# A fused attention and routed expert kernel on one core: k and v of the attention stage loaded as two partition halves, kv products over 128 rows, x written behind all loads

## The chip, the cores and the metric

The kernel runs on one core of one Trainium2 chip. The metric is device time in microseconds (us) of one execution; lower is better. The matmul engine is called PE, VectorE DVE, ScalarE ACT, GpSimd POOL and the queue that issues most DMAs SP.

## The reference

```python
# q, k, v: (8 batches, 8 heads, 576 rows, 64), float32
kv  = einsum('bhsd,bhse->bhde', k, v)          # one 64x64 matrix per batch and head
out = einsum('bhsd,bhde->bhse', q, kv)
rms = sqrt(mean(out * out, axis=-1) + 1e-06)
x   = (out / rms * g_norm) as rows of (4608, 512)      # a row per batch and place, heads side by side
logits = x @ w_gate                            # 8 experts
# greedy, largest logit first: each token goes to one expert, each expert takes 576 tokens
out[mask_e] = relu(x[mask_e] @ w1[e]) @ w2[e]
```

## The kernel before

The program has two stages with a search between them. The attention stage computes x and the logits, the search finds the first expert's threshold, and the expert stage runs two matmul layers for each of the eight experts. The change touches the attention stage alone (lines 69 to 565).

**Loads.** For each batch b and each half h of the heads, `load` (L82) brings k, v and q as one DMA of 576 KB each, so there are 48 loads. A tile holds 128 partitions: two heads of 64 partitions, nine rows of 64 values in each partition (2304 contiguous bytes). k and v of a head thus lie in 64 partitions, and a product over a head's 576 rows is nine matmuls of 64 rows. All loads go through SP; `paced` (L74) makes each wait until the third DMA before it has landed. Every tile has two buffers, so batch b+2 is asked for when batch b has been used (`again`, L398). The first twelve loads come in the order k v q k v q, twice.

**Per batch.** `prepare(b)` (L367) is a generator that is advanced between the output tiles of the batch before. It sums k^T v in `sum_kv` (L391, matmuls L395), copies the odd half out (L415), adds it to the even half (L417), copies kv into both partition halves of `kvx` on POOL (L423), transposes kv (L431, copy L433), multiplies it with the gate's weights (L442, eight matmuls of 64 weight columns, so that an output tile's logits come out of the same matmul as the tile), and turns q with PE transposes (`turn_q`, L376, matmuls L380, copies L384 and L386).

**Output tiles.** `tiles` (L453) makes four tiles of 128 rows for an even batch and five for an odd one, the fifth from two batches. For each, `one` (L464) runs eight matmuls (L479; sixteen for the fifth), ACT squares (L485) and copies (L486), DVE sums (L490). Then `scale` (L492) and `logits` (L500) finish the batch; POOL scales x (L511), for the last five tiles ACT does so at the stage's end in eight pieces per tile (L516).

**Writes.** x goes back to memory through the same SP queue and the same pacing (L520). Writes are held in a list, and a batch's end issues those that are over eight (L557); the rest stands at the end of the stage.

**Order.** The order of instructions on PE, DVE, ACT and SP is the order in which the code calls them. Small DVE jobs for the search ("chores") are placed between tiles (L545, L555). `ones` (L356) are matmuls of a 128x512 bf16 block whose result is not used; they stand at the stage's start (18), before each batch's kv (2), before the first tile (1) and before the fourth (2).

Of the kernel before, what the change touches and what calls it, by code (L numbers as in the profile page):

```python
# [7 lines left out]
FT = mybir.dt.float32  # L8
# [3 lines left out]
AL = mybir.AluOpType  # L12
# [3 lines left out]
P = 128  # L16
# [10 lines left out]
def kernel(  # L27
# [41 lines left out]

    loaded = {}  # L70
    AHEAD = 3
    issued = []

    def paced(dma):  # L74

        if len(issued) >= AHEAD:
            tc.add_manual_dep(dma.ins, issued[-AHEAD].name,
                              mybir.DependencyInfo(mybir.DependencyClass.Sync, mybir.DependencyReason.DATA),
                              reason="paced loads")
        issued.append(dma.ins)  # L80

    def load(name, b, h):  # L82

        loaded[name, b, h] = att.tile([P, NP // 2, R, D], FT, name=f"{name}_sb", tag=name + str(h), bufs=2)
        rs = slice(h * NP // 2, (h + 1) * NP // 2)
        src = {"k": k, "v": v, "q": q}[name]
        paced(nc.sync.dma_start(
            loaded[name, b, h].rearrange("p r j d -> p r (j d)"),
            src[b].rearrange("h s d -> (h s) d").rearrange("(r p j) d -> p r (j d)", r=NP, j=R)[:, rs]))

    for b in range(2):
        for h in range(2):
            for name in "kvq":
                load(name, b, h)

    ones_b = asg.tile([P, P], BF, name="ones_b")
    nc.vector.memset(ones_b, 1.0)
# [269 lines left out]
    def prepare(b):  # L367

        k_sb, v_sb, q_sb = ([loaded.pop((name, b, h)) for h in range(2)] for name in "kvq")
        q_sb = [x.rearrange("p r j d -> p (r j d)") for x in q_sb]  # L370
        NT = NP * R // 2
        qt = att.tile([P, 2, NT, HP], FT, name="qt", tag="qt", bufs=3)
        turned_q[b] = qt

        def turn_q(n):
            m = min(4, NT - 4 * n)  # L376
            t_ps = psa.tile([P, 4, P], FT, name="qt_ps", tag="tr", bufs=2)
            for x in range(m):
                h, at = divmod(4 * n + x, NT // 2)
                nc.tensor.transpose(t_ps[:, x, :], q_sb[h][:, at * P:(at + 1) * P], ident)  # L380

            to, got = qt[:, :, 4 * n:4 * n + m], t_ps[:, 0:m].rearrange("p x (l c) -> p l x c", l=2)
            if n in (1, 2):
                nc.vector.tensor_copy(to, got)  # L384
            else:
                nc.scalar.copy(to, got)  # L386


        kv_ps = psa.tile([P, 2, 512], FT, name="kv_ps", tag="kv")

        def sum_kv(r):  # L391
            for j in range(R):
                for l in range(2):
                    ls, cs = slice(l * D, (l + 1) * D), slice(j % 2 * D, (j % 2 + 1) * D)
                    nc.tensor.matmul(kv_ps[cs, l, r * D:(r + 1) * D], lhsT=k_sb[r // 2][ls, r % 2, j, :], rhs=v_sb[r // 2][ls, r % 2, j, :],  # L395
                                     start=(j < 2), stop=(j >= R - 2))

        def again(names, h):  # L398
            if b + 2 < B:
                for name in names:  # L400
                    load(name, b + 2, h)

        if b > 0:
            ones(2, kv_ps[:, 0, :])
        for r in range(2):
            sum_kv(r)
            if r:
                again("kv", 0)
            turn_q(r)
            yield  # L410
        sum_kv(2)
        sum_kv(3)
        again("kv", 1)
        odd = att.tile([D, 2, NP * D], FT, name="odd", tag="odd")
        nc.scalar.copy(odd, kv_ps[D:P, :, 0:NP * D])  # L415
        kv = att.tile([D, NP, 2, D], FT, name="kv", tag="kv")
        nc.vector.tensor_tensor(kv.rearrange("p r l d -> p l r d"),  # L417
                                kv_ps[0:D, :, 0:NP * D].rearrange("p l (r d) -> p l r d", d=D),
                                odd.rearrange("p l (r d) -> p l r d", d=D), op=AL.add)

        kvx = att.tile([P, H, W], FT, name="kvx", tag="kvx", bufs=3)
# [5 lines left out]
        turn_q(2)  # L427
        again("q", 0)
# [3 lines left out]
        kvt = att.tile([P, NP, D], FT, name="kvt", tag="kvt")  # L432
        nc.scalar.copy(kvt, t_ps)  # L433
        yield
        turn_q(3)
        if b == 0:
            nc.vector.tensor_scalar(gw.rearrange("p r l e -> p (r l e)"), in0=gw.rearrange("p r l e -> p (r l e)"),
                                    scalar1=g_col, scalar2=None, op0=AL.mult)
        w_ps = psa.tile([P, NP, 2 * E], FT, name="w_ps", tag="tr", bufs=2)
        for r in range(NP):  # L440
            for n in range(2):
                nc.tensor.matmul(w_ps[n * D:(n + 1) * D, r], lhsT=kvt[:, r, :],  # L442
                                 rhs=gw[:, r].rearrange("p l e -> p (l e)"), start=True, stop=True)
        nc.vector.tensor_copy(kvx[:, :, D:W], w_ps.rearrange("p r (l e) -> p (r l) e", l=2))
        kv_of[b] = kvx
        turn_q(4)
        again("q", 1)

    LAG = 4
    writes, late = [], []  # L450
    last_own = GC - (R + 1) // 2

    def tiles(c0, rows):  # L453


        T = len(rows)
        o_sb = att.tile([P, T, H, W], FT, name="o_sb", tag="o_sb", bufs=2)
        xo = att.tile([P, T, H, D], FT, name="xo", tag="xo", bufs=LAG + 1)
# [5 lines left out]
        def one(t, copies, fill):  # L464

            o_ps = psa.tile([P, 2, 512], FT, name="o_ps", tag="o", bufs=2)
            ones(fill, o_ps[:, 0, :])
            for r2 in range(NP // 2):
                for l in range(2):
                    for rp in range(2):  # L470
                        r = 2 * r2 + rp
                        at = [slice(h * HP, (h + 1) * HP) for h in range(2)]
                        halves = rows[t]
                        parts = [(slice(0, P), halves[0], 2)] if halves[0][0] == halves[1][0] else [
                            (at[n], half, 1) for n, half in enumerate(halves)]
                        for rows_at, (bn, j), m in parts:
                            block = R * r + j
                            ks = slice(block % 2 * D, (block % 2 + 1) * D)
                            nc.tensor.matmul(  # L479
                                o_ps[rows_at, rp, (2 * r2 + l) * W:(2 * r2 + l + 1) * W],  # L480
                                lhsT=turned_q[bn][ks, l, block // 2:block // 2 + m].rearrange("p x c -> p (x c)"),
                                rhs=kv_of[bn][ks, 2 * r + l], start=True, stop=True)
# [4 lines left out]
            if own or t != T - 2:  # L487
# [41 lines left out]
    with tc.manual_schedule(engines={PE, DVE, ACTE, SPE}):  # L529
# [3 lines left out]
        for b in range(B):  # L533
# [715 lines left out]
```

## Time and profile before

| | |
|---|---|
| median of 3 runs | 661.99 us (658.17 to 667.01) |
| the profiled execution | 660.36 us |
| its span on the core | 658.6 us |
| attention stage, start to its last output matmuls | about 0 to 123 us |
| search, first product with L646 to the expert's weights (L828) | 127.9 to 151.0 us |
| PE busy over the span | 605.8 us (92%) |
| k, v, q loads | 48 of 576 KB, median 5.8 to 6.1 us from issue to landing |
| writes of x | 16 of 512 KB and 4 of 256 KB, 4.4 and 4.0 us |

The time outside the span is 660.36 - 658.6 = 1.8 us. The stretches of ten microseconds show how the engines share the attention stage: the columns are PE, PE's weight loads, DVE, ACT and POOL busy, with counts, then the granted clock, the DMA engines' busy share and the rate.

```profile
50.00:60.00 10.00, 9.37 (x203) 7.53 (x199) 5.02 (x10) 5.80 (x12) 5.07 (x6) 1.00 0.91 294
100.00:110.00 10.00, 8.60 (x210) 7.04 (x208) 8.03 (x14) 5.46 (x11) 6.58 (x7) 1.00 0.96 362
110.00:120.00 10.00, 6.52 (x89) 5.15 (x89) 8.22 (x17) 4.48 (x11) 4.25 (x4) 0.93 0.90 336
120.00:130.00 10.00, 2.69 (x69) 2.32 (x69) 7.37 (x29) 7.90 (x29) 0.00 (x0) 0.50 0.12 49
```

PE and the DMA engines are both nearly full until 110 us. From 120 us on both are nearly idle, and the granted clock is half.

### The profile page before, as it was taken

The page shows a single profiled execution, that of the slowest core. Times are in us where ns is not written, and L with a number is a line of the kernel's source. Part 1 is how long each engine was busy: PE and PEld are TensorE (multiplying, and loading weights), DVE is VectorE, ACT ScalarE, POOL GpSimd, SP SyncE. Part 2 cuts the span into 40 slices and gives each one's busy share as a digit, 9 for nine tenths or more (in the row PEclk, how much of TensorE's full clock was granted, in tenths as well). Part 3 has the DMA queues.
Part 4 walks back from the last instruction along what each step waited for, and adds up shares of the span by engine and source line. Part 5 has one row for each costly group of instructions (what it writes and reads, how often), then busy time and mean ns, then how long its engine had stood idle before and what let it go on. Part 6 is the DMA issues. An engine that isn't in the chain of part 4 may idle for free.

```text
span 658.6 us, 12759 instructions
## 1 busy us (share of the span) xinstructions
PE 605.8 (92%) x4932; PEld 464.6 (71%) x4932; DVE 387.8 (59%) x1249; ACT 194.5 (30%) x395; POOL 389.3 (59%) x405
## 2 busy tenths in 40 slices
PE   7989998335899999999999999999999999999994
PEld 4767777232678677867786786778678867877873
DVE  4466667778678588668757956976671053123201
ACT  1555665611131223123212222231223123222300
POOL 1035434104585487749846974887388669848822
PEclk9999999657999999999999999999999999999998
DMA  8999989416306402710442072109103620721001
GB/s 270 310 315 295 292 291 340 154 50 199 128 0 204 164 33 71 257 41 33 158 171 73 1 262 99 41 0 323 46 32 100 229 72 1 279 84 37 0 9 64
DMA packets 49852, 91.02 MB, mean 138 GB/s; under 512 B 3712, under 2 KB 20096, under 8 KB 49792
## 3 DMA queue, kind: packets, MB, share of 16 engines
q1 hardware_dynamic: 43200, 71.31, 31.6%
q0 software_dynamic: 5888, 18.88, 8.3%
q8 instruction: 39, 0.64, 0.4%
q14 instruction: 21, 0.17, 0.1%
q10 hardware_dynamic: 704, 0.02, 0.1%
HBM read 71.32 MB, written 18.87 MB: 137 GB/s over the span
## 4 chain that ended last, share of the span: by engine, by line
PE 77%; DVE 9%; DMA 5%; issue 4%; ACT 3%; POOL 1%; POOLq 0%; SPq 0%; DVEq 0%; ACTq 0%
PE x_ps L1065 13%; PE x_ps L1025 11%; PE z_ps L1065 9%; PE y_ps L1065 9%; PE z_ps L1025 7%; PE y_ps L1025 7%; PE o_ps L479 4%; PE y_ps L1127 4%; PE kv_ps L395 3%; PE t_ps L969 3%; PE qt_ps L380 2%; DMA v_sb<-in_v_dram 2%; DMA q_sb<-in_q_dram 2%; PE given_ps L651 1%; PE given_ps L646 1%
## 5 line engine op out<-in xcount | busy, mean ns | idle before, releaser
L1070 ACT COPY h<-x_ps 128x288 f32<-128x288 f32 x93 | 37.2, 400 | 166.5 <-PE x_ps L1065 153.7
L1065 PE MATMUL x_ps<-xs,sw 128*128 128x288 f32 x248 | 71.3, 409 | 0.0
L875 POOL DMA_INDIRECT xg<-x_dram,ids x40 | 38.1, 952 | 51.8 <-DMA w_sb<-in_moe_w_dram 37.7
L992 POOL DMA_INDIRECT out_dram<-y_sb,outs x32 | 31.5, 983 | 55.8 <-DVE y_sb L1163 41.1
L1025 PE MATMUL x_ps<-tw,sh 128*128 128x256 f32 x256 | 61.6, 384 | 0.0
L972 ACT ACTIVATE xt<-t_ps,g_col 128x512 f32<-128x512 f32 (+1 forms) x40 | 25.7, 645 | 110.9 <-PE t_ps L969 110.9
L1065 PEld LDWEIGHTS x_ps<-xs,sw 128*128 128x128 f32 x248 | 46.2, 190 | 14.3 <-issue 1.7
L955 POOL TENSOR_TENSOR sw<-w_sb 128x256 f32<-128x256 f32 x64 | 46.8, 731 | 12.3 <-PE z_ps L1065 9.6
L1017 POOL TENSOR_TENSOR sh<-hid 128x512 f32<-128x512 f32 x32 | 40.7, 1272 | 19.9 <-ACT hid L1040 19.9
L1025 PEld LDWEIGHTS x_ps<-tw,sh 128*128 128x128 f32 x256 | 46.9, 190 | 7.1 <-issue 0.8
L1040 ACT ACTIVATE hid<-hid 128x576 f32<-128x576 f32 x64 | 43.8, 686 | 22.9 <-DVE hid L1079 13.1
L511 POOL TENSOR_TENSOR xo<-o_sb,inv 128x512 f32<-128x512 f32 x31 | 32.9, 1090 | 29.7 <-DVE inv L498 16.6
L1103 POOL TENSOR_TENSOR tw<-w_sb 128x512 f32<-128x512 f32 x32 | 40.1, 1276 | 5.0 <-DMA w_sb<-in_moe_w_dram 5.0
L479 PEld LDWEIGHTS o_ps<-kvx,qt 64*128 64x128 f32 (+1 forms) x640 | 33.7, 181 | 12.0 <-issue 7.1
L479 PE MATMUL o_ps<-kvx,qt 64*128 64x72 f32 (+1 forms) x640 | 38.9, 274 | 3.4 <-ACT o_sb L486 3.4
L1065 PE MATMUL z_ps<-xt,sw 128*128 128x288 f32 x128 | 37.8, 413 | 0.1
L1065 PE MATMUL z_ps<-xs,sw 128*128 128x288 f32 x128 | 37.0, 409 | 0.0
L1065 PE MATMUL x_ps<-xt,w_sb 128*128 128x288 f32 x124 | 36.8, 414 | 0.1
L1065 PE MATMUL y_ps<-xt,w_sb 128*128 128x288 f32 x128 | 36.9, 409 | 0.0
L1065 PE MATMUL y_ps<-xs,w_sb 128*128 128x288 f32 x128 | 36.7, 408 | 0.0
L490 DVE TENSOR_REDUCE ms<-sq 128x8 f32<-128x512 f32 x36 | 24.3, 683 | 20.1 <-ACT sq L485 19.8
L423 POOL COPY kvx<-kv 64x512 f32<-64x512 f32 x16 | 9.7, 607 | 43.9 <-DVE kv L417 26.9
(278 smaller groups left out, 1332.4 us busy)
## 6 DMA issues: line engine op xcount, KB each, us to landing
w_sb<-in_moe_w_dram SPq DMA_DIRECT2D x32, 512.0 KB, 5.7
w_sb<-in_moe_w_dram SPq DMA_DIRECT2D x8, 2048.0 KB, 14.3
k_sb<-in_k_dram SPq DMA_DIRECT2D x16, 576.0 KB, 5.8
v_sb<-in_v_dram SPq DMA_DIRECT2D x16, 576.0 KB, 5.8
q_sb<-in_q_dram SPq DMA_DIRECT2D x16, 576.0 KB, 6.1
x_dram<-xo SPq DMA_DIRECT2D x16, 512.0 KB, 4.4
x_dram<-xo SPq DMA_DIRECT2D x4, 256.0 KB, 4.0
xg<-x_dram,ids POOLq DMA_INDIRECT x40, 5.4
```

What stands on the lines that cost most here:

```text
L479: nc.tensor.matmul(o_ps[rows_at, rp, (2 * r2 + l) * W:(2 * r2 + l + 1) * W], lhsT=turned_q[bn][ks, l, block // 2:block // 2 + m].rearrange ...
L511: nc.gpsimd.tensor_tensor(xo[:, t], o_sb[:, t, :, 0:D], inv[:, t * H:(t + 1) * H].rearrange("p (h o) -> p h o", o=1).to_broadcast([P, H, D ...
L875: tokens = nc.gpsimd.indirect_dma_start(out=xg[0:nr], out_offset=None, in_=x_dram, in_offset=bass.IndirectOffsetOnAxis(ap=ids[0:nr, n:n + ...
L955: in_order(nc.gpsimd.tensor_tensor(o, x, y, op=op))
L992: put = nc.gpsimd.indirect_dma_start(out=out, out_offset=bass.IndirectOffsetOnAxis(ap=ids_of[t][0:nr, n:n + 1], axis=0), in_=y_sb[0:nr, :] ...
L1017: in_order(nc.gpsimd.tensor_tensor(o[:, ms], x[:, ms], y[:, ms], op=op))
L1025: nc.tensor.matmul(p_ps[:, n], lhsT=left[:, f, n * P:(n + 1) * P], rhs=right[:, f], start=first, stop=(f == FH - 1), skip_group_check=True)
L1040: nc.scalar.activation(both, both, ACT.Relu)
L1065: nc.tensor.matmul(p_ps, lhsT=lhs[:, r], rhs=rhs[:, r], start=(m in (1, 2, 4, 5) and r == 0), stop=(r == 1), skip_group_check=(m in (6, 7, ...
L1070: nc.scalar.copy(u, p_ps)
L1103: in_order(nc.gpsimd.tensor_tensor(o, x, y, op=AL.subtract))
L1127: nc.tensor.matmul(y_ps[l * nr:(l + 1) * nr], lhsT=hid[:, l * FH + f, a:a + nr], rhs=w2[:, l * FH + f, :], start=(f == 0), stop=(f == FH - 1))
```

## The change

- A tile of k or v holds four heads. Each head's 576 rows are cut over 128 partitions: partitions 0 to 63 hold the first five of each nine rows (1280 bytes), partitions 64 to 127 the other four (1024 bytes). A load is two DMAs of 64 partitions each; both wait for the third load before.
- `sum_kv` runs five matmuls per head, four over 128 rows and one over 64. The two heads of a pair go to the two column halves, so nothing is added afterwards: two copies, one on ACT and one on DVE, take the place of copy and add. kv's accumulator is one bank with two buffers.
- Per batch, kv comes in two pieces and not three; the turns of q move behind them, and k, v are loaded ahead of q in all batches but the first.
- kv's transpose is copied twice side by side, and the gate's part is four matmuls of 128 weight columns.
- The two `ones` before the fourth tile are gone. In odd batches the fifth tile, which needs the batch before, comes first; `qt` and `kvx` have two buffers.
- Writes of x wait until the end of batches 4 and 5, behind the last load in SP's order; `xo` has six buffers. ACT scales the last nine tiles and not five.
- The chores of the last choice before the end (columns 18 to 26) stand between the tiles of batch 6.

```diff
-    def paced(dma):
+    def paced(*dmas):
-        if len(issued) >= AHEAD:
...
+        for dma in dmas:
+            if len(issued) >= AHEAD:
...
+        issued.append(dmas[-1].ins)
...
+        if name != "q":
+            tile_of = att.tile([P, H // 2, UP, D], FT, name=f"{name}_sb", tag=name + str(h), bufs=2)
+            loaded[name, b, h] = tile_of
+            rows_of_head = src[b, h * H // 2:(h + 1) * H // 2].rearrange("h (p j) d -> p h (j d)", j=R)
+            paced(*[nc.sync.dma_start(tile_of[n * HP:(n + 1) * HP, :, 0:js.stop - js.start].rearrange("p h j d -> p h (j d)"),
+                                      rows_of_head[:, :, js.start * D:js.stop * D])
+                    for n, js in enumerate((slice(0, UP), slice(UP, R)))])
+            return
...
-    for b in range(2):
-        for h in range(2):
-            for name in "kvq":
-                load(name, b, h)
+    for b, order in enumerate(("kvqkvq", "kvkvqq")):
+        for n, name in enumerate(order):
+            load(name, b, int(name in order[:n]))
...
-        kv_ps = psa.tile([P, 2, 512], FT, name="kv_ps", tag="kv")
-
-        def sum_kv(r):
-            for j in range(R):
-                for l in range(2):
-                    ls, cs = slice(l * D, (l + 1) * D), slice(j % 2 * D, (j % 2 + 1) * D)
-                    nc.tensor.matmul(kv_ps[cs, l, r * D:(r + 1) * D], lhsT=k_sb[r // 2][ls, r % 2, j, :], rhs=v_sb[r // 2][ls, r % 2, j, :],
-                                     start=(j < 2), stop=(j >= R - 2))
+        kv_ps = psa.tile([P, 512], FT, name="kv_ps", tag="kv", bufs=2)
+
+        def sum_kv(half):
+            for r in range(half * NP // 2, (half + 1) * NP // 2):
+                for j in range(UP):
+                    ps = slice(0, P if j < R - UP else HP)
+                    for l in range(2):
+                        h = 2 * r + l - half * H // 2
+                        nc.tensor.matmul(kv_ps[l * D:(l + 1) * D, r * D:(r + 1) * D], lhsT=k_sb[half][ps, h, j, :],
+                                         rhs=v_sb[half][ps, h, j, :], start=(j == 0), stop=(j == UP - 1))
...
+        turns = [[0], [1], [2], [3, 4]] if b == 0 else [[], [0], [1, 2], [3, 4]]
...
-        nc.scalar.copy(odd, kv_ps[D:P, :, 0:NP * D])
...
+        nc.scalar.copy(kv[:, :, 1], kv_ps[D:P, 0:NP * D].rearrange("p (r d) -> p r d", d=D))
+        nc.vector.tensor_copy(kv[:, :, 0], kv_ps[0:D, 0:NP * D].rearrange("p (r d) -> p r d", d=D))
+        turn_some()
...
-            for n in range(2):
-                nc.tensor.matmul(w_ps[n * D:(n + 1) * D, r], lhsT=kvt[:, r, :],
-                                 rhs=gw[:, r].rearrange("p l e -> p (l e)"), start=True, stop=True)
+            nc.tensor.matmul(w_ps[:, r], lhsT=kvt[:, r].rearrange("p n d -> p (n d)"),
+                             rhs=gw[:, r].rearrange("p l e -> p (l e)"), start=True, stop=True)
...
-    LAG = 4
+    HELD = 6
...
-    last_own = GC - (R + 1) // 2
+    last_own = GC - R
...
-            for t in range(len(rows)):
-                one(t, copies, {0: 1, 3: 2}.get(t, 0))
+            order = range(len(rows)) if b % 2 == 0 else [len(rows) - 1] + list(range(len(rows) - 1))
+            for n, t in enumerate(order):
+                one(t, copies, 1 if n == 0 else 0, b + 1 == B and n == len(rows) - 2)
                 next(parts, None)
-                if b < 2 or t == 3 or b == 6 and t == 2:
+                if b < 2 or n == 3 or b == 6:
                     chore()
...
-            if b < B - 1:
-                chore(2 if b == 6 else 1)
-
-            while len(writes) >= 2 * LAG:
+            if b < B - 2:
+                chore()
+
+            while b in (B - 4, B - 3) and writes:
                 writes.pop(0)()
```

More of the change, by code (lines that the diff above doesn't have):

```diff
@@ L71 @@
     AHEAD = 3
+    UP = (R + 1) // 2
     issued = []
-    def paced(dma):
-        if len(issued) >= AHEAD:
[L77 to L80, printed above, removed]
-    def load(name, b, h):
+    def paced(*dmas):
+        for dma in dmas:
+            if len(issued) >= AHEAD:
+                tc.add_manual_dep(dma.ins, issued[-AHEAD].name,
+                                  mybir.DependencyInfo(mybir.DependencyClass.Sync, mybir.DependencyReason.DATA),
+                                  reason="paced loads")
+        issued.append(dmas[-1].ins)
+    def load(name, b, h):
+        src = {"k": k, "v": v, "q": q}[name]
+        if name != "q":
[6 more added lines that the diff above has]
+            return
         loaded[name, b, h] = att.tile([P, NP // 2, R, D], FT, name=f"{name}_sb", tag=name + str(h), bufs=2)
         rs = slice(h * NP // 2, (h + 1) * NP // 2)
-        src = {"k": k, "v": v, "q": q}[name]
         paced(nc.sync.dma_start(
@@ L371, in prepare @@
         NT = NP * R // 2
-        qt = att.tile([P, 2, NT, HP], FT, name="qt", tag="qt", bufs=3)
+        qt = att.tile([P, 2, NT, HP], FT, name="qt", tag="qt", bufs=2)
         turned_q[b] = qt
@@ L401, in again, with turn_some @@
                     load(name, b + 2, h)
-        if b > 0:
[L404 to L414, printed above, removed]
-        nc.scalar.copy(odd, kv_ps[D:P, :, 0:NP * D])
+        turns = [[0], [1], [2], [3, 4]] if b == 0 else [[], [0], [1, 2], [3, 4]]
+        def turn_some():
+            for n in turns.pop(0):
+                turn_q(n)
+                if n in (2, 4):
+                    again("q", n // 2 - 1)
+        if b > 0:
+            ones(2, kv_ps)
+        for half in range(2):
+            sum_kv(half)
+            again("kv", half)
+            if half == 0:
+                turn_some()
+                yield
         kv = att.tile([D, NP, 2, D], FT, name="kv", tag="kv")
[L417 to L421, printed above, removed]
+        nc.scalar.copy(kv[:, :, 1], kv_ps[D:P, 0:NP * D].rearrange("p (r d) -> p r d", d=D))
+        nc.vector.tensor_copy(kv[:, :, 0], kv_ps[0:D, 0:NP * D].rearrange("p (r d) -> p r d", d=D))
+        turn_some()
+        kvx = att.tile([P, H, W], FT, name="kvx", tag="kvx", bufs=2)
         for n in range(2):
@@ L426, in prepare @@
         yield
-        turn_q(2)
-        again("q", 0)
         t_ps = psa.tile([P, NP, D], FT, name="t_ps", tag="tr", bufs=2)
@@ L431, in prepare @@
             nc.tensor.transpose(t_ps[:, r, :], kv[:, r].rearrange("p l d -> p (l d)"), ident[0:D, 0:D])
-        kvt = att.tile([P, NP, D], FT, name="kvt", tag="kvt")
-        nc.scalar.copy(kvt, t_ps)
+        kvt = att.tile([P, NP, 2, D], FT, name="kvt", tag="kvt", bufs=1)
+        nc.scalar.copy(kvt, t_ps.rearrange("p r (o c) -> p r o c", o=1).to_broadcast([P, NP, 2, D]))
+        turn_some()
         yield
-        turn_q(3)
         if b == 0:
@@ L440, in prepare @@
         for r in range(NP):
-            for n in range(2):
-                nc.tensor.matmul(w_ps[n * D:(n + 1) * D, r], lhsT=kvt[:, r, :],
-                                 rhs=gw[:, r].rearrange("p l e -> p (l e)"), start=True, stop=True)
+            nc.tensor.matmul(w_ps[:, r], lhsT=kvt[:, r].rearrange("p n d -> p (n d)"),
+                             rhs=gw[:, r].rearrange("p l e -> p (l e)"), start=True, stop=True)
         nc.vector.tensor_copy(kvx[:, :, D:W], w_ps.rearrange("p r (l e) -> p (r l) e", l=2))
         kv_of[b] = kvx
-        turn_q(4)
-        again("q", 1)
-    LAG = 4
+        turn_some()
+    HELD = 6
     writes, late = [], []
-    last_own = GC - (R + 1) // 2
+    last_own = GC - R
     def tiles(c0, rows):
@@ L457, in tiles @@
         o_sb = att.tile([P, T, H, W], FT, name="o_sb", tag="o_sb", bufs=2)
-        xo = att.tile([P, T, H, D], FT, name="xo", tag="xo", bufs=LAG + 1)
+        xo = att.tile([P, T, H, D], FT, name="xo", tag="xo", bufs=HELD)
         ms = att.tile([P, T * H], FT, name="ms", tag="ms")
@@ L462, in tiles, with one @@
         own = c0 + T <= last_own
-        def one(t, copies, fill):
+        def one(t, copies, fill, wait):
             o_ps = psa.tile([P, 2, 512], FT, name="o_ps", tag="o", bufs=2)
@@ L486, in one @@
             copies.append(lambda: nc.scalar.copy(o_sb[:, t].rearrange("p (b h) w -> p b (h w)", b=2), o_ps[:, :, 0:NP * W]))
-            if own or t != T - 2:
+            if not wait:
                 while copies:
```

## The prediction

> **What bounds the kernel now.** I read the page's slices first, then the chain of waits for the first 190 us, then the groups by form for the first 125 us, then SP's instructions in order of time. Only the attention stage changes, so all questions are about the time at which the search starts.
>
> The slices (16.5 us each) show that two resources are nearly full together:
>
> ```profile
> PE   7989998335899999999999999999999999999994
> PEclk9999999657999999999999999999999999999998
> DMA  8999989416306402710442072109103620721001
> ```
>
> PE and DMA fill slices 1 to 7, then both fall. The clock falls with them[...]. The chain of waits (start, us, what) says which of the two sets the pace:
>
> ```profile
> 30.65 5.29 DMA q_sb<-in_q_dram
> ...
> 48.45 0.73 PE kv_ps L395 x36
> 49.18 0.59 PE qt_ps L380 x4
> 49.76 1.04 PE o_ps L479 x16
> ...
> 53.17 1.31 PE kv_ps L395 x70
> ...
> 95.50 6.05 DMA q_sb<-in_q_dram
> ...
> 114.94 1.11 DVE best L303
> 116.04 2.13 DVE over_c L335 x2
> ...
> 127.94 0.43 PE given_ps L646 x9
> ```
>
> Between 36 and 95 us the chain is PE without a load on it: 12.7 us for an even batch, 13.06 for an odd one (starts of the first output tiles in the trace: 46.80, 59.48, 72.54, 85.22, 98.28). Twice PE stands still for q, 1.87 us at 34.2 and 1.15 us at 100.4 (starts of single records). At the end the chain is DVE, and the search starts at 127.94. SP shows why q is late the second time:
>
> ```profile
> 81.90 4.52 SPq L520 DMA_DIRECT2D x_dram<-xo  x3
> 88.69 0.37 SPq L87 DMA_DIRECT2D k_sb<-in_k_dram  x1
> ...
> 99.35 35.15 SPq L520 DMA_DIRECT2D x_dram<-xo  x17
> ```
>
> Three writes stand ahead of the last batch's six loads. Between 40 and 50 us the DMA engines moved 319 GB/s, so a load of 589,824 bytes takes 1.86 us, a batch's six take 11.2, and 1.5 MB of writes about 4.9. DMA is thus only 1.5 us per batch faster than PE.
>
> The price list is in these groups (count, busy and mean ns, idle):
>
> ```profile
> L395 PE MATMUL kv_ps<-v_sb,k_sb 64*64 64x64 f32 x1152 | 23.8, 223 | 1.1 <-DMA v_sb<-in_v_dram 1.1
> L442 PE MATMUL w_ps<-gw,kvt 128*64 128x16 f32 x128 | 5.2, 212 | 0.0
> ```
>
> A product in float32 is two records. 1152 records are 144 per batch. From the chain, the second 36 records of a kv piece cost 1.31 - 0.73 = 0.58 us; the starts show them in ten rounds of up to four, 58 ns apart, on the four quarters of the array. The other 0.15 us of a piece is the change to another shape of the array.
>
> [...] No bulk transfer of the kernel before uses 64 partitions[...]. [...] kv to q's turn loses about 0.15 us, while q's turn to `ones`, both on the whole array, loses nothing (109 ns, the turn's own step). [...] turns with 128 columns start every 109 ns, kv's rounds with 64 every 58.
>
> **The change, part by part.**
>
> *kv's products.* Before: ten rounds for each of four pairs of heads, 40 per batch. After: five products by two records by two column halves, again ten rounds per pair if the column halves run together. The nearest row says they do: L442 has 128 rows and 64 columns, and its 16 records start within 0.44 us, two every 58 ns. So nothing is saved; full height replaces two row halves side by side. Bounds: together 0, one after the other 40 rounds more, 2.3 us per batch. I take 0. But the fifth product has 64 rows, so the shape changes inside a piece: three times in each of two pieces, 6 x 0.145 = 0.87 us. One piece fewer and the turn order save as much: I count 16 changes in an even batch before and after, 17 and 18 in an odd one. Sum: 0 and +0.14.
>
> *Gate's part.* Eight rounds of 58 ns (0.46 us) become eight records of 128 columns at 109 (0.87): +0.41 per batch.
>
> *Ones.* Two fewer, 216 ns apart: -0.43 per batch. They fill no gap that appears otherwise; the stage is at full clock.
>
> *Stalls.* Before, an even batch waits about 0.76 us on copies (after the transposes, and before q's last turn), an odd one 0.46. After, two turns follow the transpose directly and the second needs the bank that ACT's copy must free: that copy stands behind a square (0.60) and a copy (0.55), itself takes 0.59 for the doubled width, and ends some 1.8 us after the tile; PE arrives after 1.1. I take 0.8 in all: +0.04 and +0.34.
>
> Sum for batches 0 to 6: even batches about 0 (batch 0 -0.3, it loses a gap), three odd ones +0.5: +1.2 us.
>
> *Copies of kv.* ACT 0.58 and DVE 0.68 in series become two halves side by side. They feed POOL's copies, which are needed a batch later: nothing, covered by the next tile of 1.05 us.
>
> *Loads.* This is the disputed size. k and v become 64 DMAs of 64 partitions. Smaller pieces alone cost little: in the trace a piece of 1024 bytes takes a median of 46 ns, 2304 take 93, so 1024 + 1280 take about 101, 9% more. Lower bound: 1.86 us per load. [...] The DMA records show that they aren't in step: the sixteen completion marks of one load spread over 1.2 to 2.2 us, about as long as a load lasts. [...] I take 2.4. Then a batch's loads take 4 x 2.4 + 2 x 1.86 = 13.3, and the last lands at 2.7 (first bytes and the slow first load) + 8 x 13.3 = 109.3. SP's extra issues, 32 of 0.37 us, fit into the pace.
> At the start kv's second piece waits for four k, v loads: 4 x 0.54 = +2.2, and the work behind it is 0.4 longer.
>
> *Writes.* They no longer stand before loads, so with loads in time both q waits go: -3.0. All 20 writes (9.4 MB, at some 360 GB/s 26 us) follow the last load, and only the gather, at 155.8, needs them. ACT's pieces grow from 40 to 72, 238 ns apart: 17.2 us from 124.5, to 141.7. On SP the expert's weights (151.04) queue behind the last write, 9 us later. Nothing, by that cover.
>
> *Tail.* best and over_c (3.2 us) move ahead of batch 6's scaling on DVE. The first sum of batch 7 then waits for about 4.9 us after q's last turn instead of 6.4: -1.8 with one tile's overlap.
>
> Sum: 1.2 + 2.6 - 3.0 - 1.8 = -1.0 us against 660.36: 659.4. The median of the runs shown lies 1.6 above the profiled time, so I predict 661.
>
> **The rivals.**
>
> *B, slower: [...] loads become the bound.* At 2.8 us a load, a batch takes 14.9 us, the last q lands at 2.7 + 8 x 14.92 = 122. Behind it stand half a turn, a tile, the gate's part and two turns (3.6 us) and the tail (14.2): search at 139.8, +12 (2.7 us: +9; 3.0 us: +18). It decides from about 2.45 us per load, where 109.3 + 3.6 passes PE's own 112.7. For it: [...] PE's margin of 1.5 us. Against: the spread of marks.
>
> *C, faster: loads keep their rate and the shape changes inside kv cost nothing.* Then 7 x 0.87 = 6.1 and 2.2 more are saved: -9; one of the two alone -3 to -7. For it: only one height changes there. Against: every change of height in the trace costs.
>
> *D: the two column halves run one after the other,* 8 x 2.3 = +18. L442 speaks against it.
>
> **Chances.** A 0.42, B 0.33, C 0.20, D 0.05. A's own range is 656 to 665, B 668 to 679, C 651 to 657, D 676 to 682. The range 653 to 676 leaves out C's end, and B's and D's upper ends, about 2 in 10. 2% is 13 us, about what a measurement of this kernel can tell from no change. Only C at more than its sum gets there downward: 0.03. B's upper part and D get there upward: 0.19. Within: 0.78.
>
> **What would show it.** Right: output tiles of batch starts 12.7 and 13.5 us apart with no q or v wait on the chain after 25 us; no write in SP before the last q; kv pieces of 1.74 us; k, v landing about 2.4 us apart. B: waits for k, v or q in every batch, batch starts 14.5 us or more apart, and a DMA share near 0.95 at 220 to 260 GB/s. C: pieces of 1.31 us. D: pieces of 2.5 us or more. A gather that waits for x would make the cover of the writes wrong.

## The result and the profile after

| | before | after |
|---|---|---|
| median (executions) | 660.73 us (4) | 686.94 us (4) |
| lowest, highest | 658.17, 667.01 | 685.30, 690.03 |
| ratio, 95% interval | | 1.0393 [1.0325, 1.0461] |
| profiled execution, span | 660.36, 658.6 | 688.26, 686.5 |
| mean granted clock of that execution | 0.968 | 0.934 |
| search's first product | 127.94 | 155.89 |
| last q landed | about 103 | about 124 |

The kernel became 4% slower; 661 was predicted, with a range up to 676. The whole difference lies before the search: its first product comes 28.0 us later, and the span is 27.9 us longer. From there on nothing changes: the expert's weights are on the chain 23.7 us after that product before, 23.8 us after.

The page's slices of the kernel after (17.2 us each), with the granted clock and the DMA engines' share:

```profile
PE   5998988974489999999999999999999999999994
PEclk9699996565599999999999999999999999999998
DMA  9999999923440451271063108104520810541001
```

Two things differ from before. The DMA engines are full through the first eight slices, though the bytes of the loads are the same and the writes come later than before. And the clock falls in slice 2 and again from slice 7 on, inside the attention stage, where before it fell only at the stage's end (118.6 us). The same by stretches of ten microseconds (busy times with counts, then clock, DMA share, GB/s):

```profile
50.00:60.00 10.00, 9.04 (x113) 7.15 (x113) 5.02 (x27) 6.45 (x13) 1.21 (x2) 1.00 1.10 233
100.00:110.00 10.00, 7.86 (x144) 6.33 (x143) 4.98 (x11) 3.55 (x8) 5.43 (x6) 0.88 1.06 252
110.00:120.00 10.00, 9.75 (x64) 8.44 (x62) 3.16 (x6) 3.60 (x7) 0.00 (x0) 0.50 1.02 224
120.00:130.00 10.00, 10.00 (x99) 7.77 (x97) 6.74 (x14) 3.44 (x7) 5.41 (x5) 0.50 0.97 360
140.00:150.00 10.00, 9.01 (x110) 7.91 (x111) 6.19 (x16) 6.50 (x14) 0.00 (x0) 0.74 0.15 56
```

At 50 us the engines are wholly busy (the share adds up the times of packets, so it can pass 1) and move 233 GB/s, where before they moved 294 at a share of 0.91. At 120 us, when x is written from all 128 partitions, the same engines move 360. So it is the loads that are slow, not the engines. From 110 to 140 us PE is busy nearly all the time, at half the clock.

The chain of waits says who sets the pace (start, us, what; lines of the kernel after):

```profile
67.63 7.55 DMA v_sb<-in_v_dram
...
82.09 8.62 DMA v_sb<-in_v_dram
...
99.25 8.54 DMA q_sb<-in_q_dram
...
109.01 1.94 PE o_ps L489 x16
...
137.75 1.92 PE o_ps L489 x16
...
155.89 0.43 PE given_ps L657 x9
```

Every batch now has a load on the chain. In the trace the pair of half DMAs of a k or v load lands 2.73 us after the pair before it (median of 20), 216 GB/s, and the stage's last q at about 124. From 108 us an output tile takes 1.94 us instead of the usual 1.05. PE's instructions around that moment, with the wait before each in brackets:

```profile
104.72 1.82 PE L406 MATMUL kv_ps<-v_sb,k_sb 128*64 128x64 f32 x40 [0.75 <-DMA v_sb<-in_v_dram]
107.93 1.09 PE L389 MATMUL qt_ps<-ident,q_sb 128*128 128x128 f32 x4 [1.38 <-DMA q_sb<-in_q_dram]
108.94 1.99 PE L489 MATMUL o_ps<-kvx,qt 64*128 64x72 f32 x16
```

Two waits for loads within 4 us, and the next tile already runs at half speed (1.99 us; the tile at 102.85 us took 1.12). The trace gives half the clock from 107.6 to 145.1 us.

### The profile page after: what moved, and what is told of

It reads as the page before. It is cut to its first block, busy times and chain, and to the rows that moved or that the text cites. A ratio compares the mean times of both kernels' runs of the same rounds, so it can differ in the third digit from the quotient of the medians.

```text
span 686.5 us, 11655 instructions
## 1 busy us (share of the span) xinstructions
PE 630.7 (92%) x4340; PEld 486.3 (71%) x4340; DVE 384.5 (56%) x1249; ACT 201.9 (29%) x427; POOL 385.0 (56%) x401
## 4 chain that ended last, share of the span: by engine, by line
PE 68%; DMA 15%; DVE 7%; issue 4%; SPq 2%; ACT 1%; POOL 1%; POOLq 0%; DVEq 0%; ACTq 0%
PE x_ps L1076 12%; PE x_ps L1036 11%; PE z_ps L1076 9%; PE y_ps L1076 8%; DMA v_sb<-in_v_dram 7%; PE z_ps L1036 7%; PE y_ps L1036 7%; DMA k_sb<-in_k_dram 6%; PE y_ps L1138 4%; PE o_ps L489 3%; PE t_ps L980 3%; SPq L91 1%; DMA q_sb<-in_q_dram 1%; PE given_ps L662 1%; PE qt_ps L389 1%
## 5 line engine op out<-in xcount | busy, mean ns | idle before, releaser
L886 POOL DMA_INDIRECT xg<-x_dram,ids x40 | 38.2, 954 | 64.0 <-DMA w_sb<-in_moe_w_dram 49.9
L521 POOL TENSOR_TENSOR xo<-o_sb,inv 128x512 f32<-128x512 f32 x27 | 28.8, 1097 | 52.0 <-DVE inv L508 52.0
L489 PE MATMUL o_ps<-kvx,qt 64*128 64x72 f32 (+1 forms) x640 | 46.3, 305 | 0.2 <-ACT o_sb L496 0.2
L489 PEld LDWEIGHTS o_ps<-kvx,qt 64*128 64x128 f32 (+1 forms) x640 | 40.8, 210 | 7.9 <-issue 5.9
L406 PE MATMUL kv_ps<-v_sb,k_sb 128*64 128x64 f32 (+1 forms) x640 | 33.7, 253 | 8.9 <-DMA v_sb<-in_v_dram 8.9
L406 PEld LDWEIGHTS kv_ps<-v_sb,k_sb 128*64 128x64 f32 (+1 forms) x640 | 27.7, 156 | 17.8 <-issue 13.7
```

The source lines that it names most:

```text
L406: nc.tensor.matmul(kv_ps[l * D:(l + 1) * D, r * D:(r + 1) * D], lhsT=k_sb[half][ps, h, j, :], rhs=v_sb[half][ps, h, j, :], start=(j == 0), ...
L489: nc.tensor.matmul(o_ps[rows_at, rp, (2 * r2 + l) * W:(2 * r2 + l + 1) * W], lhsT=turned_q[bn][ks, l, block // 2:block // 2 + m].rearrange ...
L521: nc.gpsimd.tensor_tensor(xo[:, t], o_sb[:, t, :, 0:D], inv[:, t * H:(t + 1) * H].rearrange("p (h o) -> p h o", o=1).to_broadcast([P, H, D ...
L886: tokens = nc.gpsimd.indirect_dma_start(out=xg[0:nr], out_offset=None, in_=x_dram, in_offset=bass.IndirectOffsetOnAxis(ap=ids[0:nr, n:n + ...
```

## The experiments

Five theories were to be told apart. P: a DMA into one half of the partitions is slower than one into all 128, and k and v are in such DMAs. Q: the smaller pieces or the number of DMAs are what is slow. K: waits of a microsecond or more make the clock fall, and the fall costs more than the wait. T: the tail's jobs on DVE. R: what is lost lies in the order of the loads or in the short fifth product. Where a run's kernel is called by a name, the name is that of its heading. Medians of the kernel before, taken beside the runs below, were 659.8 to 662.7 us.

**before_halves.** The kernel before, and nothing but its k and v loads cut into two DMAs of 64 partitions, with pieces of 2304 bytes as they were.

```diff
+            rows = src[b].rearrange("(r l) (p j) d -> l p r (j d)", l=2, j=R)
+            paced(*[nc.sync.dma_start(loaded[name, b, h][l * HP:(l + 1) * HP].rearrange("p r j d -> p r (j d)"),
+                                      rows[l][:, rs]) for l in range(2)])
```

> The kernel before with one edit: each load of k and v is two DMAs of 64 partitions (the heads with even numbers, then those with odd numbers), pieces of 2304 bytes as before. Theory P [...]: a k or v load takes 2.7 to 2.8 us and not 1.86, a batch 14.7 us of DMA, search no earlier than 148 us, time 680 to 692. Rival Q (the changed kernel's loads are slow because its pieces are smaller and its DMAs more): the pieces are unchanged and 32 more issues of 0.4 to 0.6 us are hidden, so 658 to 664.

Measured: 685.48 us (685.16 to 686.16), ratio 1.0368 [1.0296, 1.0440]. Two stretches of its profile, in columns as above:

```profile
70.00:80.00 10.00, 9.17 (x179) 7.21 (x173) 6.97 (x16) 5.62 (x12) 4.03 (x5) 1.00 0.98 245
90.00:100.00 10.00, 9.32 (x102) 7.06 (x97) 5.18 (x11) 3.92 (x8) 4.80 (x5) 0.54 1.02 227
```

This one part, put alone into the kernel before, brings 24 us of the 26 (against 661.62 for before beside it). The rate is 245 GB/s from 70 to 80 us at a full DMA share, where before moved 309, although no piece is smaller than before; a half DMA takes about 1.3 us, and the median piece of 2304 bytes 159 ns in the place of 93. Q falls and P stands. The clock falls here too (0.54 in the second row).

**after_even_odd.** The kernel after, with the same two DMAs per load laid on even and odd partitions, so that each is spread from the first partitions to the last; the fifth product runs over 128 rows, POOL having written zeros where there is no row.

```diff
-            paced(*[nc.sync.dma_start(tile_of[n * HP:(n + 1) * HP, :, 0:js.stop - js.start].rearrange("p h j d -> p h (j d)"),
+            nc.gpsimd.memset(tile_of[:, :, UP - 1], 0.0)
+            paced(*[nc.sync.dma_start(tile_of.rearrange("(p n) h j d -> n p h j d", n=2)[n][:, :, 0:js.stop - js.start].rearrange("p h j d -> p h (j d)"),
...
-                    ps = slice(0, P if j < R - UP else HP)
+                    ps = slice(0, P)
```

> The changed kernel with one edit in its loads: the first five of each nine rows go to the even partitions and the other four to the odd ones, so each DMA still has 64 partitions, 256 pieces of 1280 or 1024 bytes, but spread over the whole memory; the fifth product then runs over 128 rows, with zeros in the odd partitions from a small fill on GpSimd. P: a k or v load takes 1.9 to 2.1 us, the last q lands by 102, no load is waited for after 40 us, the clock stays full to about 118, kv pieces 1.31 us: time 650 to 659. Q: loads stay at 2.75 us, time 683 to 689.

Measured: 668.05 us (665.45 to 671.48), ratio 1.0119 [1.0036, 1.0202]. The number of DMAs, their order and their bytes are those of after, and 19 of the 26 us are gone (the fifth product over full rows has a part in this: it saves 0.88 us of PE's time per batch):

```profile
50.00:60.00 10.00, 8.95 (x156) 7.48 (x155) 6.05 (x13) 6.16 (x12) 6.48 (x10) 1.00 0.97 311
```

311 GB/s in the place of 233, and the last q lands at about 101. The time of single pieces in the traces shows where the loads lose it (pieces that started between 25 and 100 us):

```
kernel            piece       median   75 ns or more
after             1280 bytes   99 ns   80%
after_even_odd    1280 bytes   55 ns    5%
after             1024 bytes   82 ns   71%
after_even_odd    1024 bytes   46 ns    1%
```

What was expected of the loads came; the time, forecast at 650 to 659, did not, and the clock held to 112 us and not to 118. Two things remained. At the start batch 0's first tile came at 22.60 us, 3.8 later than before, after a wait for v of 2.6 us and the clock at half for 3.4 and 6.8 us. From there on the distance to before stays 4.0 to 4.2 us (first tiles of batches 2, 4, 6: 50.76, 76.60, 102.43 against 46.80, 72.54, 98.28). So kv over 128 rows, even without shape changes in it, saves nothing per batch. The second thing is late, on the chain:

```profile
106.62 2.14 DVE over_c L345 x2
...
110.63 0.33 DVE kv L433
111.01 0.47 PE t_ps L444 x4
...
113.17 1.92 PE o_ps L490 x16
```

The copy of kv is now a DVE instruction, and it stands behind the chores moved into batch 6. PE waits 1.6 us for it, and then its tile takes 1.92 us: the clock has fallen (0.61 from 110 to 120 us).

**after_rows.** The kernel after, its short product included, with the rows dealt out otherwise: four rows to each of the 128 partitions in one DMA, the last 64 rows to partitions 0 to 63 in another.

```diff
+            heads = src[b, h * H // 2:(h + 1) * H // 2]
+            paced(nc.sync.dma_start(tile_of[:, :, 0:UP - 1].rearrange("p h j d -> p h (j d)"),
+                                    heads[:, 0:(UP - 1) * P].rearrange("h (p j) d -> p h (j d)", j=UP - 1)),
+                  nc.sync.dma_start(tile_of[0:HP, :, UP - 1], heads[:, (UP - 1) * P:].rearrange("h p d -> p h d")))
```

> The kernel after, with the rows dealt out in another way: a k or v load is one DMA of four rows for each of the 128 partitions (512 KB, pieces of 1024 bytes) and one of the last 64 rows into partitions 0 to 63 (64 KB, pieces of 256 bytes). The same result; the products, the short fifth one among them, the loads' order and the writes are those of after. Only a ninth of the bytes of k and v goes into one half at a time. Theory P [...]: a load takes 1.9 to 2.1 us, a batch's loads about 11.8, the last q lands near 100 and PE sets the pace again. Against the even and odd partitions (668) the short product's shape changes come back, 0.87 us per batch, seven batches, about 6: 668 to 676. Rival R (what after loses lies in the number of DMAs, in their order or in the short products): this kernel keeps all three, so 682 or more. If small pieces of 256 bytes are what is slow (as slow each as those of 1024), a load takes 2.3 or more and the result lies between.

Measured: 680.69 us median of four that spread from 670.23 to 689.83 at mean clocks of 0.958 down to 0.921, so no ratio is given: two lie in P's forecast (670.23 and 675.37), two in R's (686.02 and 689.83, at the lowest clocks). The profiled execution is the one of 670.23 and kept its clock from 31.6 to 134.0 us; it is read here, the median decides nothing. In it no load is on the chain after 25 us, the rate is 288 to 303 GB/s from 50 to 80 us, and pieces of 1024 bytes take 46 ns there. P again, and R falls as far as the loads go. But with PE alone setting the pace, this profile shows what else after costs. Two batches take 27.58 us (first tiles at 56.35 and 83.94), against 25.74 before and 25.83 in after_even_odd. Its groups of PE by form, 40 to 110 us (busy us, mean ns, idle before):

```profile
L389 PE MATMUL qt_ps<-ident,q_sb 128*128 128x128 f32 x96 | 16.4, 287 | 4.7 <-ACT kvt L445 4.2
L406 PE MATMUL kv_ps<-v_sb,k_sb 128*64 128x64 f32 x320 | 13.7, 228 | 0.0
L406 PE MATMUL kv_ps<-v_sb,k_sb 64*64 64x64 f32 x80 | 6.6, 242 | 0.0
```

and the chain of one batch:

```profile
64.73 0.63 ACT o_sb L496
65.36 0.50 ACT kvt L445
65.91 0.66 PE qt_ps L389 x4
```

The second turn of q waits for the bank that ACT's doubled copy frees, once in every batch. From the starts of PE's records over two batches, before and after_rows (two records of `ones` are missing in the second trace; their 0.22 us each are counted as `ones`):

```
us in two batches        before   after_rows
kv's products             5.54     7.02
turns of q, with waits    5.24     7.58
output tiles, with waits  9.03     8.89
transposes, with waits    1.38     0.67
gate's part, with waits   1.80     1.83
ones                      2.76     1.60
sum                      25.74    27.58
```

**after_fill.** The kernel after, from batch 4 on with 12 unused matmuls of 128x256 where PE waits for v.

```diff
+            if half and b >= 4:
+                for _ in range(12):
+                    nc.tensor.matmul(kv_ps[:, 256:512], lhsT=ones_b, rhs=wide[:, 0:256], start=True, stop=True)
             sum_kv(half)
```

> The changed kernel with twelve more unused matmuls of a 128x256 bf16 block (1.3 us) before each batch's second kv piece from batch 4 on, where TensorE waits for loads. Theory K (the two waits of 1.0 and 1.6 us at 104 to 108 let the clock fall to half, and that costs a further 12 to 14 us): the clock stays at full until the search, the search starts near 143, time 672 to 677. Rival (the clock falls for another reason, or its fall is free because loads set the pace): clock at half from about 108 again, 686 to 692, or a full clock and the time unchanged.

Measured: 686.22 us (676.95 to 695.35), ratio 1.0378 [1.0278, 1.0477]. The profiled execution is the one of 676.95, as K expects, with the full clock from 101.8 to 139.4 us after a fall of 3.4 us. The others had mean clocks of 0.949 to 0.924. Filling the waits thus doesn't keep the clock for certain: inconclusive for K.

**after_ones.** The kernel after, with the two `ones` ahead of the fourth tile put back.

```diff
-                one(t, copies, 1 if n == 0 else 0, b + 1 == B and n == len(rows) - 2)
+                one(t, copies, {0: 1, 3: 2}.get(n, 0), b + 1 == B and n == len(rows) - 2)
```

> The changed kernel with one edit: the two unused matmuls before each batch's fourth tile are back. Theory O (the fewer ones are why the clock, once it fell at 107 us, stayed at half to 145): the clock falls there as before but is full again within 7 to 14 us, mean clock 0.945 or more and not 0.93, time 674 to 681. Rival (loads alone set the time, ones don't matter): mean clock 0.93, 685 to 691.

Measured: 684.50 us (675.67 to 685.28), ratio 1.0361 [1.0312, 1.0411]; four of five executions lie at 684.5 to 685.3 with clocks of 0.942 to 0.944, against 0.925 to 0.934 in after. Beside the kernel before of its own runs (659.82) it is 24.7 us slower, after was 26.2: the missing `ones` are not what costs the time. The profiled execution is the fifth, 675.67 us at 0.967, and it is useful by accident, as the kernel after with its clock held:

```profile
100.00:110.00 10.00, 8.55 (x161) 6.78 (x159) 5.21 (x12) 4.54 (x11) 5.43 (x6) 1.00 1.02 254
110.00:120.00 10.00, 9.04 (x116) 6.81 (x114) 5.34 (x13) 5.58 (x12) 0.60 (x1) 1.00 1.09 224
```

The loads are as slow as in after (224 to 254 GB/s). PE waits for v and q at the same place as in after, by the same view 0.66 us at 105.1 and 0.79 at 107.7 in the place of 0.75 and 1.38, and the clock stays at 1.00. Its search starts at 142.91: 15.0 us later than before, and 13.0 us earlier than after. That splits the 28 us into loads with the rest of the change, and clock, as far as two single executions can: this kernel has two `ones` more per batch than after.

**even_odd_fill** and **even_odd_fill_act.** after_even_odd, with 24 unused matmuls of 128x256 ahead of batch 0's second kv piece; the second one also copies kv's even half on ACT and not on DVE.

```diff
+            if half and b == 0:
+                for _ in range(24):
+                    nc.tensor.matmul(kv_ps[:, 256:512], lhsT=ones_b, rhs=wide[:, 0:256], start=True, stop=True)
...
-        nc.vector.tensor_copy(kv[:, :, 0], kv_ps[0:D, 0:NP * D].rearrange("p (r d) -> p r d", d=D))
+        nc.scalar.copy(kv[:, :, 0], kv_ps[0:D, 0:NP * D].rearrange("p (r d) -> p r d", d=D))
```

> The changed kernel with loads on even and odd partitions, which took 668, and 24 unused matmuls of 128x256 before batch 0's second kv piece, where TensorE waits 2.9 us. Theory (about half of the 6 us that are left over the kernel before come from the clock's fall at 13 to 27 us): the clock holds there, batch 0's first tile starts at 19.5 to 20.5 and not at 22.6, time 664 to 666. Rival: no effect, 668.

> even_odd_fill with one more edit: the copy of kv's even half is ScalarE's and not VectorE's, which comes 1.8 us late in batch 6 behind the search's comparisons. Theory (that delay opens the gap at 109 us and drops the clock before the last tiles): no gap at 109 us, the clock is full to the last tiles, time 657 to 661. Rival (what is left is in the products of kv or of the gate, 6 us over the batches): 664 or more.

Measured: 664.44 us (661.21 to 671.28), ratio 1.0064 [1.0035, 1.0094], and 663.28 us (658.66 to 667.79), ratio 1.0045 [1.0021, 1.0069]. The first is as forecast: batch 0's first tile comes at 20.12 and not at 22.60, with the clock full from 5.1 to 70.0 us. The second lies between theory and rival, and the two intervals overlap; whether the late copy matters for the time stays open. Neither reaches before.

**before_late_x.** The kernel before with the part that stands for itself: writes of x behind all loads, ACT scaling the last nine tiles, the fifth tile first in odd batches, `qt` in two buffers.

```diff
-    LAG = 4
+    HELD = 6
...
-    last_own = GC - (R + 1) // 2
+    last_own = GC - R
...
-            while len(writes) >= 2 * LAG:
+            while b in (B - 4, B - 3) and writes:
```

> The kernel before with the change's writes alone: x is held until the end of batches 4 and 5, six buffers for it, ScalarE scales nine tiles, the fifth tile of odd batches comes first and q's turned tile has two buffers (needed for room). Theory: no write stands before a load, the wait for q at 95 to 101 us goes, 656 to 660. Rival W (holding x back costs at the end: the writes or the pieces on ScalarE delay the gather): 665 or more.

Measured: 660.70 us (656.38 to 673.01), ratio 0.9966 [0.9937, 0.9996]. The writes are hidden, as predicted, and the part gains about 0.3%; the median lies just above the forecast of 656 to 660. The wait for q at 100.4 us is gone, the one in batch 1 is not.

**before_fewer_ones.** The kernel before without the two `ones` ahead of the fourth tile.

```diff
-                one(t, copies, {0: 1, 3: 2}.get(t, 0))
+                one(t, copies, {0: 1}.get(t, 0))
```

> The kernel before with one part of the change: the two unused matmuls before each batch's fourth tile are gone. If they only cost their 0.43 us per batch, loads are waited for a little longer instead: 659 to 662. If they hold the clock: falls to half between 30 and 118 us and 664 to 672.

Measured: 662.67 us (656.23 to 675.07), ratio 0.9997 [0.9968, 1.0027]. The 3.0 us that their time sums to (7 x 0.43) are not gained. In the profiled execution, 665.14 us, the clock was at half from 82.4 to 99.5 us, which is what was expected if the `ones` hold it. The median lies between the two forecasts, so whether they do stays open.

**late_x_fill** and **late_x_tail_fill.** before_late_x with 14 unused matmuls of 128x256 where PE, during batch 1's tiles, waits for q of batch 2; the second one also moves the chores as after does.

```diff
+            if b == 2 and r == 0:
+                for _ in range(14):
+                    nc.tensor.matmul(kv_ps[:, 0, 256:512], lhsT=ones_b, rhs=wide[:, 0:256], start=True, stop=True)
             turn_q(r)
...
-                if b < 2 or n == 3 or b == 6 and n == 2:
+                if b < 2 or n == 3 or b == 6:
...
-            if b < B - 1:
-                chore(2 if b == 6 else 1)
+            if b < B - 2:
+                chore()
```

> The kernel before with the writes behind all loads, and with 14 matmuls of 128x256 whose result is not used (some 1.5 us) ahead of q's first turn of batch 2, where PE otherwise waits 2.0 us for q at 34.4 us and the clock then was half from 38.2 to 45.0 in the profiled execution. Theory K (a wait of a microsecond or two makes the clock fall, and what a run loses beyond the wait itself is the clock): the clock stays full past 100 us, the runs gather near 656 to 658 and the median falls from 660.7 to about 658. Rival: the clock falls in about as many runs as before, for a reason outside the wait; the median stays at 660 to 662.

> The kernel before with the writes behind all loads, the 14 matmuls of the run beside it, and the small DVE jobs for the search placed as in after (all done before the scaling of batch 6). Theory T of the prediction (the last jobs stand ahead of the search's first product, and moving them brings 1.8 us): 1 to 2 us below the run beside it, 655 to 658. Rival U, from the even and odd partitions, where a copy of kv stood behind these jobs on DVE: the jobs delay batch 7's kv copy as much as they shorten the end, so the same as beside it or later, and the clock may fall.

Measured: 658.28 us (656.56 to 664.20), ratio 0.9956 [0.9930, 0.9981], and 658.26 us (655.60 to 671.25), ratio 0.9942 [0.9908, 0.9976]. PE's instructions at that place, first in before_late_x:

```profile
36.43 0.63 PE L380 MATMUL qt_ps<-ident,q_sb 128*128 128x128 f32 x4 [1.77 <-DMA q_sb<-in_q_dram]
...
40.25 1.99 PE L479 MATMUL o_ps<-kvx,qt 64*128 64x72 f32 x16
```

and in late_x_fill:

```profile
34.06 1.70 PE L411 MATMUL kv_ps<-wide,ones_b 128*128 128x256 bf16 x14
36.06 0.63 PE L380 MATMUL qt_ps<-ident,q_sb 128*128 128x128 f32 x4 [0.30 <-DMA q_sb<-in_q_dram]
36.62 1.11 PE L482 MATMUL o_ps<-kvx,qt 64*128 64x72 f32 x16
```

q comes at about the same time in both. In the first, the tile at 40.25 takes 1.99 us, at half the clock (38.2 to 45.0 us); in the second the clock stays full until 120.7. That agrees with K, and the median fell as forecast, but the intervals of the three ratios overlap. In the profiled execution of late_x_tail_fill q landed later, PE still waited 1.77 us behind the 14 matmuls, and the clock stayed: after a wait of that length it fell in one execution (before_late_x) and not in the other. T shows no gain beside late_x_fill here. Both are faster than before by 0.4 to 0.6%; they are the fastest of the kernels tried.

## Why the prediction was wrong

**The loads: the failed step.** The prediction took 2.4 us for a k or v load. Like the 2.7 to 3.0 of rival B this was my estimate and not shown: no trace of before has a load into 64 partitions. Measured: 2.73, or 216 GB/s. What failed was the argument for the lower figure. The sixteen marks of one load spread over 1.2 to 2.2 us, and I read this as engines that are out of each other's way half of the time. The pieces don't bear that out. In after the piece's size tells its half of the partitions (1280 bytes below, 1024 above), and 80% and 71% of the pieces took 75 ns or more, not half.

One explanation would be that pieces hold each other up when most of them go to one half: at the instants between 31 and 99 us with at least eight such pieces under way, on average 82% of them were in the same half. The trace speaks against this. Of the pieces of 1280 bytes that had under 60% of the pieces under way in their own half, 98% took 75 ns or more; of those that had 90% or more, 62%. Pieces are not slower when their half is more crowded. So it is shown that a DMA confined to one half is slow (before_halves, 245 GB/s in the place of 309) and that spreading it over both cures it (after_even_odd, 311 in the place of 233). Why its single pieces take 99 ns is open: the records don't name the engine of a piece.

This is the size of rival B, which the prediction lets decide from 2.45 us: its last q (122) and its search (139.8) stand beside 124 and, with the clock held, 142.9. By the prediction's own sums the loads stood at that point already: at 2.4 us, 109.3 + 3.6 = 112.9 is past PE's 112.7, and each 0.1 us more on 32 loads adds 3.2.

**The clock: a cost that no case had.** The prediction wrote "the stage is at full clock" and used it for the `ones` alone. All four executions of after had mean clocks of 0.925 to 0.934, and in the profiled one PE worked through most of batches 5 and 6 at half speed. Beside the execution of after_ones that kept its clock this is 13.0 of the 28.0 us. It took the time past B's upper end. The clock didn't return with the work: PE was busy again from 16.6 us and the clock returned at 22.2; from 25.6 us it was at half for 6.8 us and from 107.6 for 37.5, with PE 97% to 100% busy in the three stretches from 110 to 140 us.

In all 13 traces every complete stretch at one clock lasts a whole number of steps of 3.413 us; in after, from 5.2 us on, 3, 2, 1, 2, 22, 11, 2 and 10 of them. The length of a wait alone doesn't decide what happens at a step's end. The fall followed waits of 0.75 and 1.38 us here, 1.62 in after_even_odd and 1.77 in before_late_x, but not the wait of 1.77 in late_x_tail_fill, and not this one in before, after which the clock stayed full to 118.6 us:

```profile
36.08 0.63 PE L380 MATMUL qt_ps<-ident,q_sb 128*128 128x128 f32 x4 [1.65 <-DMA q_sb<-in_q_dram]
```

In after most of the two waits fell into one step (104.15 to 107.56 us, 1.59 us of it idle); in the execution of after_ones that kept its clock they fell into two, 0.66 and 0.79 us. Where waits lie among the steps may thus matter, which no run tests. Which wait brings the clock down, and why it stays down so long, is open.

**Batches, +1.2 for seven.** Undersized. In after_rows a pair of batches takes 1.84 us more than before, not 0.5, or 6.4 us for seven. The kv piece of 1.74 us was right (1.754 in after_rows, 1.315 in after_even_odd without the shape changes). The change of the gate's part was right by itself, 0.91 us, but not as a loss: before needs as much with its waits. Mis-sized was the term for the stalls, "I take 0.8 in all": between q's first and second turn 1.06 us are lost for ACT's copy, and 0.24 us more in the last turns, 1.3 a batch. Over seven batches that is about 3.5 of the missing 5.2 us. Changes of shape elsewhere didn't save what the prediction's count of 16 and 16 says; how much of the rest is theirs was not separated. The 0.43 us per batch for the `ones` came in after_rows, but before_fewer_ones gained nothing by them.

**Start, +2.6.** Too small. Batch 0's first tile came 8.4 us later in after, 7.2 in after_rows, 3.8 in after_even_odd, 1.4 in even_odd_fill. The loads are slower and the order heavier, as the prediction said. Around the wait for v (4.70 us, to 16.64 us in after) the clock was at half as well, from 15.4 to 22.2 us.

**Tail, -1.8, and the second wait for q, -1.15.** About right in their sum. after_rows is 13.2 us behind before at batch 6's first tile and 9.5 at the search: -3.7 against -2.95.

**Writes: nothing.** Right. SP's writes in after:

```profile
121.14 47.58 SPq L530 DMA_DIRECT2D x_dram<-xo  x20
```

They queue behind the last q until 168.7 us; the gather comes at 184 and doesn't wait for them.

**Rivals C and D.** C (pieces of 1.31 us, loads at full rate) didn't happen in after, and after_even_odd, which has both, was still not faster than before. D (pieces of 2.5 us) is refuted by 1.754.

So of the 28 us 13.0 are clock, as far as the two executions tell. The other 15.0 can't be split by subtraction: after_rows, where PE alone sets the pace, is 9.5 us behind before (batches and start, less the tail), but where the loads set the pace, as in after, PE's own losses in part hide behind them. The half DMAs cost 24 us by themselves in before_halves, with the falls of the clock that came there.

## What to carry to other kernels

Cutting a layout at partition 64 made two slow DMAs out of a fast one here (245 GB/s in before_halves, 309 in before). A spread of landing times was no evidence that the two would stay out of each other's way; the time of single pieces and a run with the cut alone settled it. Deal the rows out so that nearly all bytes go to all partitions (288 to 303 GB/s in after_rows), or interleave the two DMAs on even and odd partitions (307 to 312 in after_even_odd). And where PE is near full and the loads near their limit, price a new wait twice: by itself, and with the work behind it at half the clock (13.0 of the 28.0 us here, as far as two executions tell).

## What the runs showed of the hardware

A pair of half-partition DMAs in a steady stream got 216 GB/s in after. Between 50 and 80 us all loads together got 233 to 252 there, and 307 to 312 with the same DMAs on even and odd partitions (after_even_odd). A DMA of 64 partitions took SP about 0.60 us to issue and not the 0.37 of one of 128 (before), with 128 pieces (before_halves) as with 256 (after). A kv piece with three changes of the array's shape inside it took 1.754 us (after_rows), one without them 1.315 (after_even_odd): 0.44 us, 0.146 a change. The clock changed only at steps of 3.413 us (85 complete stretches in 13 traces). It stayed at half for 37.5 us in after, with PE 97% to 100% busy from 110 to 140 us. Of five executions of after_ones one had a mean clock of 0.967, the others 0.942 to 0.944.
